# 128-token output tiles, early weighing of the last logit pair, and slot outputs replicated by their own products

## The chip, the cores and the metric

The kernel runs on one core of one Trainium2 chip. The time is device microseconds of one execution; the median of three executions of the kernel before is 542.49 us (540.43 to 543.66). The core's five engines run side by side, each in the order of its own instructions: TensorE (PE, products and their weight loads PEld), VectorE (DVE), ScalarE (ACT), GpSimd (POOL) and SyncE (SP, which only issues DMAs here). [...]

## The reference

Three layers in float32, with 2304 tokens (4 batches of 576) and a width of 512:

```
p_packed = attn(p, k, v);  a = attn(q, p_packed, p_packed)      # 8 heads, 32 packed queries
x   = a as tokens x 512
y   = sum_e prob[t, e] * (relu(x @ w1[e]) @ w2[e])              # 4 experts, hidden 1024
logits = y @ phi                                                # 32 slots
slot_in = softmax over tokens(logits).T @ y                     # 32 slots x 512
slot_out = relu(slot_in[e] @ m1[e]) @ m2[e]                     # 8 experts, 4 slots each
out = softmax over slots(logits) @ slot_out                     # 2304 x 512
```

The first softmax of the last layer runs over all 2304 tokens, so nothing behind slot_in can start before the last token's logits are known.

## The kernel before, in words

**Main loop.** It goes over batches b, four column blocks n of the hidden layer, halves kf and experts e (one step each, `sl`). A step makes h (L473, `mm1`), takes its relu into ht on ScalarE (L477), turns ht into hn on VectorE (L483, `flip_h`) and weighs hn with the experts' probabilities on GpSimd (L484). y itself is never formed: the logits are summed from ht with wphi = w2 @ phi (L500, `logits`), in two PSUM tiles lg, one for each pair pr of experts, and the slot sums are taken over hn (`pool_slots`, L611, tile sl) and meet w2 only at the end. ORDER writes down in which order a step issues its parts; in the last step it is logits, softmax, flip, attention, slot sums.

**Softmax of a batch.** `softmaxes(b)` is a generator, advanced by one `yield` a step: transposes of the two lg tiles into ls (L529), one multiplication of ls by the probabilities (L530), fold products that add the experts (L544, tile lt, PE), transposes into lt (L550), row maximum (L555), running maximum m_run and its negation nm (L557, L563), exponential with row sums (L565), transpose into dpt (L572). With dpt the slot sums of this batch can run. Between two of the last steps 16 products of the identity (L939, "warm") are put on TensorE.

**The stream of weights.** Chunks of w2 (16), m1 (32) and m2 (16, then 16 of 384 columns and 4 of 128 columns) are loaded in this order by SyncE (`load_chunk`, L715), each into the next of 39 buffers. The last 16 of these lie in hn, the input of the last slot sums, and come free piece by piece (ENDS) as `pool_slots(3, ...)` runs. Up to eight loads are under way at a time.

**The last part**, in order: slot sums sl of the last batch and their addition into tacc (L631); transposes tt (L961) and slot inputs si = tt @ w2 (L989); hid = relu(si @ m1) (L1026), between whose products `turn_c` prepares the combination weights ct, split into a high and a low part so that products in float32r keep their accuracy; transposes of hid into hm (L1047, L1049), where zeros keep the experts apart; so = hm @ m2 (L1074, `project`): once for experts 0 to 3 in all 512 columns, then for experts 4 to 7 in 384 columns and in 128 columns. The two are added on VectorE (L1094), a product with the selector matrix sel (L1096) places the 32 slots four times into 128 rows, a copy and a subtraction (L1098, L1099) make rr, whose lower 64 rows hold the rounding rest. An output tile is ct @ rr (L1112) for 96 tokens, drained by ScalarE and VectorE in turn (L1065), and stored with SyncE (L1119): 12 stores of 96 partitions by two rows of 384 columns, then 4 of 96 partitions by six rows of 128 columns, 288 KB each.

Of the kernel before, what the change touches and what calls it, by code (L numbers as in the profile page):

```python
# [18 lines left out]
def tile_packed_attention_moe_softmoe(  # L19
# [32 lines left out]
    NJ = NBLK // 3  # L52
# [65 lines left out]
    m_run = const.tile([128, NB], F32, name="m_run")  # L118
# [91 lines left out]
    def selectors(sel):  # L210
        for c in range(4):
            for s in range(2):
                pool.tensor_copy(
                    sel[:, 32 * c + 16 * s : 32 * c + 16 * s + 16].rearrange(
                        "p (x s) -> p x s", x=4
                    ),
                    ident.rearrange("p (x r) -> p x r", x=4)[:, :, 4 * s : 4 * s + 4],
                )
# [301 lines left out]
    def softmaxes(b):  # L520
# [5 lines left out]

        ls = sx(f"ls{b}", blocks)
        for pr in range(2):
            dve.transpose(out=ls[:, halves[pr], :], in_=wide(lg_t.pop((b, pr))))  # L529
        dve.tensor_tensor(  # L530
            out=ls, in0=ls,
            in1=dpe[:, b].rearrange("p r x -> p (r x)").unsqueeze(2).to_broadcast(blocks),
            op=ALU.mult,
        )
        yield
        own = slice(32 * b, 32 * b + 32)
        cc = c_sb[own]
        lt = sx(f"lt{b}", blocks)
        pss = []
        for hf in range(2):  # L540
            ps = tr_ps(f"lt{b}{hf}")
            r = slice(64 * hf, 64 * hf + 64)
            for pr in range(2):
# [11 lines left out]
        dve.tensor_reduce(out=mx, in_=flat, axis=AX.X, op=ALU.max)  # L555
        if b:
            dve.tensor_tensor(  # L557
                out=m_run[:, b : b + 1], in0=mx, in1=m_run[:, b - 1 : b], op=ALU.max
            )
        else:  # L560
            dve.tensor_copy(m_run[:, 0:1], mx)
        nm = small.tile([128, 1], F32, tag="nm", name=f"nm{b}", bufs=1)
        dve.tensor_scalar_mul(nm, m_run[:, b : b + 1], -1.0)  # L563
# [73 lines left out]
    def turn_c(ct):  # L637
        cf = soft.tile([128, S], F32, tag="sx", name="cf", bufs=2).rearrange(
            "p (x t) -> p x t", t=32
        )  # L640
        dve.transpose(out=cf, in_=c_sb)
        for b in range(NB):
            own = slice(32 * b, 32 * b + 32)
            for y0, ny in ((0, 2), (2, 1)):
                m = ny * NJ * 32
                ps = tr_ps(f"ct{b}{y0}")
# [5 lines left out]
                src = ps[:, :m].rearrange("p (y j t) -> p y j t", y=ny, t=32)  # L652
                dst = ct[:, b].rearrange("p j (t y) -> p y j t", y=3)[:, y0 : y0 + ny]
                for y in range(ny):
                    act.copy(dst[:, y], src[:, y])
                    for r in (slice(32, 64), slice(96, 128)):
                        dve.tensor_tensor(
                            out=dst[r, y], in0=src[r, y],
                            in1=dst[r, y].bitcast(F32), op=ALU.subtract,
                        )  # L660
                yield

    chunks = []
    for x in range(0, NFT, 2):
        for e in range(NE):
            chunks.append(
                w2[e, 128 * x : 128 * x + 256, :].rearrange("(x p) d -> p x d", p=128)
            )
# [4 lines left out]
    for x in range(0, NFT, 2):  # L673
        for e in range(4):
            chunks.append(
                m2[e, 128 * x : 128 * x + 256, :].rearrange("(x p) d -> p x d", p=128)
            )
    for d0, dw in PARTS:
        nx = CHUNK // dw
        for x in range(0, NFT, nx):  # L680
            for e in range(4):
                chunks.append(
                    m2[4 + e, 128 * x : 128 * (x + nx), d0 : d0 + dw].rearrange(
                        "(x p) d -> p x d", p=128
                    )
                )
# [50 lines left out]
    with tc.manual_schedule():  # L737
# [88 lines left out]
        flq = None  # L826
# [17 lines left out]
        for sl in range(nslot + 1):  # L844
# [62 lines left out]
            def step_logits():  # L907
                nonlocal sm_gen
# [40 lines left out]
        sel = rest(0)[:, :128]  # L949
        selectors(sel)  # L950
# [4 lines left out]
        ct = fin.tile([128, NB, NJ, 96], F32R, name="ct")  # L955
        for i in range(2):
            ps, ps2 = tr_ps(f"tt{i}a"), tr_ps(f"tt{i}b")
            for j in range(4):
                o = 128 * (4 * (2 * i + j // 2) + j % 2)
                for el in range(2):  # L960
                    pe.transpose(  # L961
                        (ps if j < 2 else ps2)[:, 256 * (j % 2) + 128 * el :][:, :128],
                        tacc[:, o + 256 * el : o + 256 * el + 128],
# [47 lines left out]
        cgen = turn_c(ct)  # L1011
# [31 lines left out]
        for i in range(2):  # L1043
            ps = tr_ps(f"hidt{i}")
            for j in range(4):
                o = 512 * i + 128 * j
                pe.transpose(ps[:, 128 * j : 128 * j + 128], hid[:, o : o + 128], ident)  # L1047
            for s in range(2):
                (act.copy if i else dve.tensor_copy)(  # L1049
                    hm[s][:, 4 * i : 4 * i + 4, :, 4 * s : 4 * s + 4].rearrange(  # L1050
                        "p a b c -> p (a b) c"
                    ),
                    ps.rearrange("p (a c) -> p a c", c=32)[:, :, 4 * s : 4 * s + 4],
# [13 lines left out]
        def project(so, s, dw):  # L1067
            nonlocal ck
            nx = CHUNK // dw
            for x in range(0, NFT, nx):  # L1070
                cks = [chunk_t.pop(ck + e) for e in range(4)]
                for xl in range(nx):
                    for e in range(4):
                        pe.matmul(  # L1074
                            so[32 * e : 32 * e + 32, :dw],
                            hm[s][:, x + xl, e, :],
                            cks[e][:, dw * xl : dw * xl + dw],
                            start=(x + xl == 0),
                            stop=(x + xl == NFT - 1),
                            tile_position=(0, 32 * e),  # L1080
                        )
# [3 lines left out]

        so = mm_ps("so")
        project(so, 0, DM)
        so_sb = rest(3)[:, :DM]
        act.copy(so_sb, so)
        for d0, dw in PARTS:  # L1090
            so = mm_ps(f"so{d0}")
            project(so, 1, dw)
            h = slice(d0, d0 + dw)
            dve.tensor_tensor(out=so_sb[:, h], in0=so[:, :dw], in1=so_sb[:, h], op=ALU.add)  # L1094
            sr = tr_ps(f"sr{d0}")
            pe.matmul(sr[:, :dw], sel, so_sb[:, h], start=True, stop=True)  # L1096
            rr = fin.tile([128, dw], F32R, name=f"rr{d0}")
            act.copy(rr, sr[:, :dw])  # L1098
            dve.tensor_tensor(  # L1099
                out=rr[64:128], in0=sr[64:128, :dw], in1=rr[64:128].bitcast(F32),  # L1100
                op=ALU.subtract,
            )
            nb, nt = 512 // dw, min(CHUNK // dw, NJ)
            for b in range(NB):
                rows = out[b * S : (b + 1) * S, h].rearrange("(r j) d -> r j d", j=NJ)
                for j0 in range(0, NJ, nt):
                    ob = out_tile()
                    for j in range(j0, j0 + nt, nb):
                        m = min(nb, j0 + nt - j)
                        ps = mm_ps(f"o{d0}_{b}_{j}")  # L1110
                        for jl in range(m):
                            pe.matmul(  # L1112
                                ps[:96, dw * jl : dw * jl + dw], ct[:, b, j + jl, :], rr,
                                start=True, stop=True,
                            )
                        drain(
                            ob[:96, dw * (j - j0) : dw * (j - j0 + m)], ps[:96, : dw * m]
                        )
                    (act if (d0, b) == (PARTS[-1][0], NB - 1) else sp).dma_start(  # L1119
                        rows[:, j0 : j0 + nt, :],  # L1120
                        ob[:96, : dw * nt].rearrange("p (j d) -> p j d", d=dw),
                    )
# [30 lines left out]
```

## Time and profile before

| | |
|---|---|
| median of three executions | 542.49 us |
| profiled execution | 541.67 us, span 539.6 us |
| busy, share of the span | PE 92%, DVE 56%, ACT 44%, POOL 46% |
| last fifth of the span | see the DMA line of the rows below |
| HBM read and written | 98.52 and 4.72 MB |
| chain that ended last | PE 65%, DVE 11%, DMA 8%, ACT 8% |

The page gives averages over the span: a busy share of 92% says nothing of the last 100 us by itself. A DMA share can exceed 1, since the times of packets that overlap on one engine are added. "Idle before" is the time in which an engine had nothing to do before an instruction, with what ended it.

### The profile page before, as it was taken

Reading aid. Unit: us, or ns where it says so; the run is one execution under the profiler, and the core shown is the slowest. Engines: PE = TensorE matmul, PEld = TensorE weight load, DVE = VectorE, ACT = ScalarE, POOL = GpSimd, SP = SyncE. Lnnn points to the kernel's source line nnn. Section 1 sums busy time; section 2 is a strip of 40 time slices with the busy share of each in tenths; the row PEclk is TensorE's granted clock in tenths of the full one; section 3 lists DMA queues with packets and bytes.
Section 4 is the critical chain, followed back from the end, with each engine's and each line's share of the span. In section 5 each row is a group of like instructions: output and inputs, shape, how many; then the busy total and the mean of one; then the engine's idle time right before and its main releaser. Section 6 shows DMA issues by size and latency. Waiting matters only on the chain.

```text
span 539.6 us, 12853 instructions
## 1 busy us (share of the span) xinstructions
PE 497.0 (92%) x5356; PEld 346.1 (64%) x5356; DVE 300.1 (56%) x559; ACT 240.0 (44%) x548; POOL 248.5 (46%) x310
## 2 busy tenths in 40 slices
PE   6898999999999999999998999999999887998883
PEld 5776787877865777877556777865878753222132
DVE  6265555747767575569755756567545425360051
ACT  3857464656452457455234565541454312120041
POOL 8412446697632667795236486732565512000000
PEclk9999999999999999999999999999999997998996
DMA  8998156253430443624215422640686459999998
GB/s 277 366 373 295 53 165 193 84 170 106 137 117 1 149 145 107 217 82 126 76 44 178 150 80 79 223 169 2 199 296 249 153 205 412 408 388 382 368 251 241
DMA packets 70873, 104.06 MB, mean 193 GB/s; under 512 B 4432, under 2 KB 50256, under 8 KB 70816
## 3 DMA queue, kind: packets, MB, share of 16 engines
q1 hardware_dynamic: 66992, 93.20, 50.2%
q0 software_dynamic: 3232, 9.75, 5.8%
q8 instruction: 42, 0.69, 0.5%
q10 hardware_dynamic: 592, 0.29, 0.2%
q14 instruction: 15, 0.12, 0.1%
HBM read 98.52 MB, written 4.72 MB: 191 GB/s over the span
## 4 chain that ended last, share of the span: by engine, by line
PE 65%; DVE 11%; DMA 8%; ACT 8%; issue 3%; POOL 3%; SPq 0%; POOLq 0%; DVEq 0%; ACTq 0%
PE h L473 30%; PE sl L611 7%; PE lg L500 5%; PE g L443 5%; DMA hn<-in_moe_w_dram 3%; ACT etm L336 3%; PE hid L1026 3%; PE pv L346 3%; PE sb L297 3%; PE sa L297 2%; DMA k<-in_k_dram 2%; DMA ck<-in_moe_w_dram 2%; PE si L989 1%; DVE hn L483 1%; PE w2t L251 1%
## 5 line engine op out<-in xcount | busy, mean ns | idle before, releaser
L473 PE MATMUL h<-a,g 128*128 128x288 f32 x1536 | 226.0, 301 | 2.5 <-POOL a L410 1.5
L473 PEld LDWEIGHTS h<-a,g 128*128 128x128 f32 x1536 | 208.0, 188 | 28.3 <-issue 22.3
L484 POOL TENSOR_TENSOR hn<-hn,dp_sb 128x576 f32<-128x576 f32 x128 | 151.6, 1191 | 123.1 <-DVE hn L483 118.8
L477 ACT ACTIVATE ht<-h 128x288 f32<-128x288 f32 x256 | 103.7, 412 | 149.1 <-PE h L473 148.8
L483 DVE STREAM_TRANSPOSE hn<-ht 128x576 f32<-128x576 f32 x128 | 96.6, 760 | 56.6 <-ACT ht L477 56.5
L455 DVE TENSOR_TENSOR g<-g,g 128x512 fp32r<-128x512 f32 x64 | 41.1, 684 | 26.6 <-ACT g L454 26.6
L611 PE MATMUL sl<-hn,dpt 32*32 32x512 f32 x1152 | 48.1, 597 | 2.3 <-DVE dpt L572 2.0
L454 ACT CAST g<-g 128x512 fp32r<-128x512 f32 x64 | 34.3, 588 | 21.1 <-PE g L443 21.0
L500 PE MATMUL lg<-ht,wphi 128*32 128x288 f32 x512 | 37.8, 412 | 0.0
L443 PE MATMUL g<-w,gl 64*32 64x512 f32 x512 | 35.7, 601 | 0.4 <-ACT ht L477 0.2
L611 PEld LDWEIGHTS sl<-hn,dpt 32*32 32x32 f32 x1152 | 21.0, 103 | 22.3 <-issue 13.3
L500 PEld LDWEIGHTS lg<-ht,wphi 128*32 128x32 f32 x512 | 13.5, 109 | 32.7 <-issue 25.5
L346 PE MATMUL pv<-etm,v 128*64 128x64 f32 x468 | 19.0, 225 | 6.7 <-ACT etm L336 2.0
L410 POOL TENSOR_TENSOR a<-a,a 64x576 fp32r<-64x576 f32 x14 | 19.9, 1424 | 9.6 <-ACT a L409 8.9
L336 ACT COPY etm<-et 32x288 f32<-32x288 f32 x52 | 22.3, 428 | 2.3 <-DVE et L330 1.1
L346 PEld LDWEIGHTS pv<-etm,v 128*64 128x64 f32 x468 | 16.2, 137 | 10.7 <-ACT etm L336 5.6
L1074 PE MATMUL so<-hn,tacc 128*32 128x384 f32 (+1 forms) x80 | 18.4, 586 | 2.7 <-DMA hn<-in_moe_w_dram 2.7
L378 DVE STREAM_TRANSPOSE nat<-sb 128x288 f32<-128x288 f32 x14 | 6.8, 483 | 25.3 <-PE sb L297 25.3
L629 DVE TENSOR_TENSOR tacc<-sl,tacc 128x512 f32<-128x512 f32 (+2 forms) x32 | 15.3, 544 | 9.4 <-PE sl L611 9.4
L256 ACT COPY hn<-w2t 128x512 f32<-128x512 f32 x32 | 17.2, 589 | 6.0 <-PE w2t L251 5.9
L251 PE MATMUL w2t<-ident,hn 128*128 128x128 f32 x128 | 17.5, 279 | 2.4 <-ACT hn L256 1.6
L631 DVE SCALAR_TENSOR_TENSOR tacc<-tacc,rsc,sl 128x384 f32<-128x384 f32 (+2 forms) x20 | 9.2, 527 | 17.3 <-PE sl L611 17.3
(180 smaller groups left out, 506.6 us busy)
## 6 DMA issues: line engine op xcount, KB each, us to landing
w<-in_moe_w_dram SPq DMA_DIRECT2D x32, 1024.0 KB, 5.3
hn<-in_moe_w_dram SPq DMA_DIRECT2D x42, 512.0 KB, 9.8
ck<-in_moe_w_dram SPq DMA_DIRECT2D x42, 512.0 KB, 9.0
hn<-in_moe_w_dram SPq DMA_DIRECT2D x14, 384.0 KB, 8.5
q<-in_q_dram POOLq DMA_DIRECT2D x12, 288.0 KB, 3.2
out_dram<-ob SPq DMA_DIRECT2D x11, 288.0 KB, 4.4
k<-in_k_dram POOLq DMA_DIRECT2D x10, 288.0 KB, 3.3
v<-in_v_dram POOLq DMA_DIRECT2D x10, 288.0 KB, 3.4
```

Source lines behind the costliest of these rows:

```text
L297: pe.matmul(ps[:, :HS], lhs[:, j, :], t[:, :, j, :], start=(j == 0), stop=(j == 1))
L336: act.copy(etb[hf % len(etb)][r, h % 2, :, 32 * (h // 2) : 32 * (h // 2) + 32], et[r, HB * hf : HB * hf + HB, :],)
L346: pe.matmul(pv[64 * par : 64 * par + 64, :64], vn[:, x, :], etb[hf % len(etb)][:, par, x, :], start=(hf == 0 and x == 0), stop=(hf == 1 an ...
L443: pe.matmul(pss[g][32 * ((c + 2 * g) % 4) : 32 * ((c + 2 * g) % 4) + 32, :], gl[b % 2][r, c, :], t[r, c], start=True, stop=True, tile_posi ...
L454: act.copy(hi, pss[g])
L455: dve.tensor_tensor(out=lo, in0=pss[g], in1=hi.bitcast(F32), op=ALU.subtract)
L473: pe.matmul(ps[:, :HS], gg[:, l, g, e % 2, fs], r[:, ts], start=(g == 0 and t == 0), stop=(g == 1 and t == 2),)
L477: act.activation(out=ht[:, ts], in_=ps[:, :HS], func=AF.Relu)
L483: dve.transpose(out=own, in_=unturned.pop((n, kf, e)).rearrange("p (x t) -> p x t", t=32))
L484: pool.tensor_tensor(out=own, in0=own, in1=dp_sb[:, n // NU, :, e].unsqueeze(2).to_broadcast([128, NBLK, 32]), op=ALU.mult,)
L500: pe.matmul(lg_t[b, pr][32 * c : 32 * c + 32, :HS], wphi[:, 2 * i + kf, 32 * e : 32 * e + 32], ht_t[n, kf, e][:, HS * hf : HS * hf + HS], ...
L611: pe.matmul(pss[f][c : c + 32, :], dpt[r, x, :], hn[r, p0 : p0 + NU, x, 2 * ep : 2 * ep + 2].rearrange("p n e k f -> p n (e k f)"), start= ...
```

## The change

- `softmaxes` of the last batch begins when the first lg tile is complete: pair 0 is transposed and multiplied then (`weigh`, `times`), pair 1 after the last logits; the fold products of pair 0 stand ahead of those of pair 1 in TensorE's order. The running maximum is kept negated (n_run), in one instruction. The last batch's exponential and its transpose into dpt are made in two halves, and its row sum is a reduction on VectorE behind them.
- The chunks of w2 and of m2 place rows differently: partition p takes neighbouring rows of the matrix (of m2 the rows 8p to 8p+7, in pieces). The transposes of tacc and hid take columns with a step of 2 or 8 to fit.
- hm holds each slot column four times, so that `project` gives the 128 rows that the selector product gave. Both groups of experts add up in the same two PSUM tiles (sos), which makes the first `project` two products (384 and 128 columns) instead of one of 512. The addition, so_sb and the selector product go. rr is made by a copy (rh) and one operation with a mask per partition (`lows`, 0 or -1), and ct likewise, with the matrix `perm` in place of fold.
- A partition now holds 18 neighbouring tokens of the output; ct has 128 columns a product. There are 9 stores of 128 partitions by two rows of 384 columns and 3 of 128 by six rows of 128 columns, 384 KB each.

```diff
-    NJ = NBLK // 3
+    OUT_X = {384: 2, 128: 6}
...
-    def selectors(sel):
+    def spread(perm, lows):
+        to = perm.rearrange("p (e c s i) -> p e c s i", e=4, c=4, s=2)
+        src = fold[:, 0].rearrange("p (s e i) -> p s e i", s=2, e=4)
         for c in range(4):
             for s in range(2):
...
+                pool.tensor_copy(to[:, :, c, s, :], src[:, s])
+        for k, w in enumerate((16, 32)):
+            dve.tensor_reduce(
+                out=lows[:, k : k + 1],
+                in_=ident.rearrange("p (a b) -> p a b", b=w)[:, :, w // 2 :],
+                axis=AX.XY, op=ALU.add,
+            )
+        dve.tensor_scalar_mul(lows, lows, -1.0)
...
+        last = b == NB - 1
         ls = sx(f"ls{b}", blocks)
...
         own = slice(32 * b, 32 * b + 32)
         cc = c_sb[own]
         lt = sx(f"lt{b}", blocks)
+
+        def weigh(pr):
+            dve.transpose(out=ls[:, halves[pr], :], in_=wide(lg_t.pop((b, pr))))
+
+        def times(prs):
+            xs = slice(halves[prs[0]].start, halves[prs[-1]].stop)
+            dve.tensor_tensor(
+                out=ls[:, xs], in0=ls[:, xs],
+                in1=dpe[:, b, prs[0] : prs[-1] + 1].rearrange("p r x -> p (r x)")
+                .unsqueeze(2).to_broadcast([128, HB * len(prs), 32]),
+                op=ALU.mult,
+            )
+
         pss = []
...
+
+        def folded(pr):
+            for hf in range(2):
+                if not pr:
+                    pss.append(tr_ps(f"lt{b}{hf}"))
+                r = slice(64 * hf, 64 * hf + 64)
                 pe.matmul(
-                    ps[:, :HS], fold[r].rearrange("p c t -> p (c t)"), ls[r, halves[pr], :],
+                    pss[hf][:, :HS], fold[r].rearrange("p c t -> p (c t)"),
+                    ls[r, halves[pr], :],
                     start=(pr == 0), stop=(pr == 1), tile_position=(64 * hf, 0),
                 )
-            pss.append(ps)
+
+        if last:
+            weigh(0)
+            times((0,))
+            yield "first"
+            weigh(1)
+            times((1,))
+            folded(0)
+        else:
+            weigh(0)
+            weigh(1)
+            times((0, 1))
+        yield
+        if not last:
+            folded(0)
+        folded(1)
...
+        nm = n_run[:, b : b + 1]
         if b:
-            dve.tensor_tensor(
-                out=m_run[:, b : b + 1], in0=mx, in1=m_run[:, b - 1 : b], op=ALU.max
+            dve.scalar_tensor_tensor(
+                out=nm, in0=mx, scalar=-1.0, in1=n_run[:, b - 1 : b],
+                op0=ALU.mult, op1=ALU.min,
             )
         else:
...
+            dve.tensor_scalar_mul(nm, mx, -1.0)
         sm = small.tile([128, 1], F32, tag="lsm", name=f"lsm{b}", bufs=1)
-        act.activation(out=flat, in_=flat, func=AF.Exp, bias=nm, accum_out=sm)
+        if last:
+            for x in halves:
+                act.activation(out=lt[:, x], in_=lt[:, x], func=AF.Exp, bias=nm)
+        else:
+            act.activation(out=flat, in_=flat, func=AF.Exp, bias=nm, accum_out=sm)
         rs = None
         if b:
             rs = small.tile([128, 1], F32, tag="rsc", name=f"rsc{b}", bufs=1)
-            act.activation(out=rs, in_=m_run[:, b - 1 : b], func=AF.Exp, bias=nm)
+            act.activation(
+                out=rs, in_=n_run[:, b - 1 : b], func=AF.Exp, bias=nm, scale=-1.0
+            )
         yield
         dpt = soft.tile([128, NBLK, 32], F32, tag="dpt", name=f"dpt{b}", bufs=1)
-        dve.transpose(out=dpt, in_=lt)
+        for x in halves if last else (slice(0, NBLK),):
+            dve.transpose(out=dpt[:, x], in_=lt[:, x])
+        if last:
+            dve.tensor_reduce(out=sm, in_=flat, axis=AX.X, op=ALU.add)
...
+            for x0 in range(0, NBLK, HB):
+                m = HB * 32
+                ps = tr_ps(f"ct{b}{x0}")
                 pe.matmul(
-                    ps[:, :m], fold[own].rearrange("p c t -> p (c t)"),
-                    cf[own, NJ * y0 : NJ * (y0 + ny), :],
+                    ps[:, :m], perm[own], cf[own, x0 : x0 + HB, :],
                     start=True, stop=True, tile_position=(32 * b, 0),
                 )
...
+                src = ps[:, :m].rearrange("p (x t) -> p x t", t=32)
+                dst = ct[:, x0 : x0 + HB, own]
+                act.copy(dst, src)
+                dve.scalar_tensor_tensor(
+                    out=dst, in0=dst.bitcast(F32), scalar=lows[:, 0:1], in1=src,
+                    op0=ALU.mult, op1=ALU.add,
+                )
...
-                m2[e, 128 * x : 128 * x + 256, :].rearrange("(x p) d -> p x d", p=128)
+                m2[e].rearrange("(p x) d -> p x d", x=NFT)[:, x : x + 2, :]
...
+                    m2[4 + e, :, d0 : d0 + dw].rearrange("(p x) d -> p x d", x=NFT)[
+                        :, x : x + nx, :
+                    ]
...
+                    if ln == NB * NU - 1 and lk == 0:
+                        sm_last = softmaxes(NB - 1)
+                        next(sm_last)
                     if ln % NU == NU - 1 and lk == 1:
-                        sm_gen = softmaxes(ln // NU)
+                        sm_gen = sm_last if ln == NB * NU - 1 else softmaxes(ln // NU)
...
+                    hm[s][:, 4 * i : 4 * i + 4].rearrange(
+                        "p a b (c u) -> p (a b) c u", u=8
+                    )[:, :, :, 4 * s : 4 * s + 4],
+                    ps.rearrange("p (a c) -> p a c", c=32)[:, :, 4 * s : 4 * s + 4]
+                    .unsqueeze(2).to_broadcast([128, 16, 4, 4]),
...
-        def project(so, s, dw):
+        sos = [
+            ps_lg.tile([128, 512], F32, tag="lg", name=f"so{d0}")[:, :dw] for d0, dw in PARTS
+        ]
+
+        def project(s, n, w, parts):
             nonlocal ck
-            nx = CHUNK // dw
-            for x in range(0, NFT, nx):
+            for x in range(0, NFT, n):
                 cks = [chunk_t.pop(ck + e) for e in range(4)]
...
+                for xl in range(n):
+                    for so, o, dw in parts:
+                        for e in range(4):
+                            pe.matmul(
+                                so[32 * e : 32 * e + 32],
+                                hm[s][:, x + xl, e, :],
+                                cks[e][:, w * xl + o :][:, :dw],
+                                start=(s == 0 and x + xl == 0),
+                                stop=(s == 1 and x + xl == NFT - 1),
+                                tile_position=(0, 32 * e),
+                            )
                 ck += 4
...
+        project(0, 2, DM, [(so, *pt) for so, pt in zip(sos, PARTS)])
+        for so, (d0, dw) in zip(sos, PARTS):
+            project(1, CHUNK // dw, dw, [(so, 0, dw)])
             h = slice(d0, d0 + dw)
...
+            rh = fin.tile([128, dw], F32R, name=f"rh{d0}")
             rr = fin.tile([128, dw], F32R, name=f"rr{d0}")
...
+            act.copy(rh, so)
+            dve.scalar_tensor_tensor(
+                out=rr, in0=rh.bitcast(F32), scalar=lows[:, 1:2], in1=so,
+                op0=ALU.mult, op1=ALU.add,
+            )
+            nb, nt = 512 // dw, OUT_X[dw]
+            rows = out[:, h].rearrange("(p x) d -> p x d", x=NBLK)
+            for x0 in range(0, NBLK, nt):
+                ob = out_tile()
+                for x in range(x0, x0 + nt, nb):
+                    m = min(nb, x0 + nt - x)
+                    ps = mm_ps(f"o{d0}_{x}")
+                    for xl in range(m):
+                        pe.matmul(
+                            ps[:, dw * xl : dw * xl + dw], ct[:, x + xl, :], rr,
+                            start=True, stop=True,
                         )
...
+                    drain(ob[:, dw * (x - x0) : dw * (x - x0 + m)], ps[:, : dw * m])
+                (act if d0 and x0 + nt == NBLK else sp).dma_start(
+                    rows[:, x0 : x0 + nt, :],
+                    ob[:, : dw * nt].rearrange("p (x d) -> p x d", d=dw),
```

## Rows read from the trace of the kernel before

**Rows 1.** The page's 40 equal slices: busy tenths of the DMA engines.
```profile
DMA  8998156253430443624215422640686459999998
```

**Rows 2.** Stretches: from:to, length, busy us (instructions) per engine, clock, DMA share, GB/s.
```profile
420.00:428.00 8.00, 8.00 (x68) 7.04 (x66) 3.38 (x6) 3.35 (x9) 4.88 (x5) 1.00 0.37 133
436.00:439.00 3.00, 3.00 (x100) 1.64 (x84) 0.00 (x0) 0.00 (x0) 0.00 (x0) 1.00 0.02 5
446.00:472.00 26.00, 21.30 (x150) 8.49 (x154) 12.02 (x39) 4.46 (x13) 4.86 (x5) 0.87 1.03 410
476.00:493.00 17.00, 15.47 (x107) 4.90 (x109) 6.40 (x15) 3.47 (x9) 0.00 (x0) 0.90 1.05 386
497.00:509.00 12.00, 10.22 (x47) 2.23 (x46) 0.00 (x0) 0.59 (x1) 0.00 (x0) 1.00 1.07 373
513.00:518.00 5.00, 3.50 (x15) 0.81 (x14) 0.56 (x1) 0.26 (x1) 0.00 (x0) 1.00 0.98 260
518.00:521.00 3.00, 2.09 (x9) 1.32 (x9) 2.02 (x4) 1.77 (x5) 0.00 (x0) 1.00 0.59 161
522.00:532.00 10.00, 8.63 (x103) 6.12 (x101) 5.77 (x14) 5.59 (x12) 0.00 (x0) 0.92 0.98 297
534.00:538.00 4.00, 0.00 (x0) 0.00 (x0) 0.00 (x0) 0.00 (x0) 0.00 (x0) 0.50 0.92 235
```

**Rows 3.** TensorE's weight loads, 490 to 515 us: us waited, times, longest.
```profile
PEld so L1074 <- DMA hn<-in_moe_w_dram: 12.1, 14, 1.3
...
PEld so L1074 <- DMA ck<-in_moe_w_dram: 3.8, 5, 1.2
```

**Rows 4.** SyncE's waits, 405 to 445 us: us waited, times, longest.
```profile
SPq L715 <- PE sl L611: 8.7, 1, 8.7
```

**Rows 5.** Chain of waits from the last logits to dpt: start, us, what.
```profile
429.35 0.49 DVE ls L529
...
429.86 0.77 DVE ls L530
...
430.68 1.25 PE lt L544 x8
...
431.95 0.86 DVE lt L550 x2
...
433.61 0.17 DVE m_run L557
...
433.81 0.17 DVE nm L563
...
434.00 0.88 ACT lt L565 x2
...
434.89 0.79 DVE dpt L572
```

**Rows 6.** Chain of waits behind the last 384-wide weight: start, us, what.
```profile
514.59 1.49 PE so L1074 x10
...
516.18 0.57 DVE hn L1094
...
516.79 0.93 PE sr L1096 x2
```

**Rows 7.** Instructions in order of time, 425 to 449 us: start, us, what, idle.
```profile
427.73 0.44 DVE L529 STREAM_TRANSPOSE ls<-lg 128x288 f32<-128x288 f32 x1
...
428.17 0.41 ACT L477 ACTIVATE ht<-h 128x288 f32<-128x288 f32 x1 [0.39 <-PE h L473]
...
430.54 0.77 DVE L483 STREAM_TRANSPOSE hn<-ht 128x576 f32<-128x576 f32 x1
...
431.39 1.19 POOL L484 TENSOR_TENSOR hn<-hn,dp_sb 128x576 f32<-128x576 f32 x1 [2.32 <-DVE hn L483]
...
438.22 10.51 SPq L715 DMA_DIRECT2D hn<-in_moe_w_dram  x12
```

**Rows 8.** Instructions in order of time: the output products of the 384 columns.
```profile
518.87 6.37 PE L1112 MATMUL o<-rr,ct 128*96 128x384 f32 x24 [1.16 <-DVE rr L1099]
```

More of the change, by code (lines that the diff above doesn't have):

```diff
@@ L525, in wide @@
             return ps[:, :HS].rearrange("p (x t) -> p x t", t=32)
+        last = b == NB - 1
         ls = sx(f"ls{b}", blocks)
-        for pr in range(2):
-            dve.transpose(out=ls[:, halves[pr], :], in_=wide(lg_t.pop((b, pr))))
-        dve.tensor_tensor(
[L531 to L535, printed above, removed]
         own = slice(32 * b, 32 * b + 32)
@@ L643, in turn_c @@
             own = slice(32 * b, 32 * b + 32)
-            for y0, ny in ((0, 2), (2, 1)):
-                m = ny * NJ * 32
-                ps = tr_ps(f"ct{b}{y0}")
+            for x0 in range(0, NBLK, HB):
+                m = HB * 32
+                ps = tr_ps(f"ct{b}{x0}")
                 pe.matmul(
-                    ps[:, :m], fold[own].rearrange("p c t -> p (c t)"),
-                    cf[own, NJ * y0 : NJ * (y0 + ny), :],
+                    ps[:, :m], perm[own], cf[own, x0 : x0 + HB, :],
                     start=True, stop=True, tile_position=(32 * b, 0),
                 )
[L652 to L660, printed above, removed]
+                src = ps[:, :m].rearrange("p (x t) -> p x t", t=32)
[5 more added lines that the diff above has]
+                )
                 yield
@@ L825, in tile_packed_attention_moe_softmoe @@
         post, lgq = [], []
-        flq = None
+        flq, sm_last = None, None
         sm_gen, att_gens, ready, soon = None, [], -1, 0
@@ L907, in step_logits @@
             def step_logits():
-                nonlocal sm_gen
+                nonlocal sm_gen, sm_last
                 if sl < 4:
@@ L948, in tile_packed_attention_moe_softmoe @@
         fin = ctx.enter_context(tc.tile_pool(name="fin", bufs=1, reuse_waits="tile"))
-        sel = rest(0)[:, :128]
-        selectors(sel)
+        perm = rest(0)[:, :128]
+        lows = small.tile([128, 2], F32, tag="lows", name="lows", bufs=1)
+        spread(perm, lows)
         st2 = [rest(1 + i).rearrange("p (c x s) -> p c x s", c=2, s=32) for i in range(2)]
@@ L1010, in tile_packed_attention_moe_softmoe @@
             )
-        cgen = turn_c(ct)
+        cgen = turn_c(ct, perm, lows)
         for s in range(2):
@@ L1045, in tile_packed_attention_moe_softmoe @@
             for j in range(4):
-                o = 512 * i + 128 * j
-                pe.transpose(ps[:, 128 * j : 128 * j + 128], hid[:, o : o + 128], ident)
+                pe.transpose(
+                    ps[:, 128 * j : 128 * j + 128],
+                    hid.rearrange("p (f x) -> p x f", x=NFT)[:, 4 * i + j],
+                    ident,
+                )
             for s in range(2):
                 (act.copy if i else dve.tensor_copy)(
[L1050 to L1053, printed above, removed]
+                    hm[s][:, 4 * i : 4 * i + 4].rearrange(
[3 more added lines that the diff above has]
+                    .unsqueeze(2).to_broadcast([128, 16, 4, 4]),
                 )
@@ L1084, in project @@
                     load_chunk()
[L1086 to L1092, printed above, removed]
+        project(0, 2, DM, [(so, *pt) for so, pt in zip(sos, PARTS)])
+        for so, (d0, dw) in zip(sos, PARTS):
+            project(1, CHUNK // dw, dw, [(so, 0, dw)])
             h = slice(d0, d0 + dw)
-            dve.tensor_tensor(out=so_sb[:, h], in0=so[:, :dw], in1=so_sb[:, h], op=ALU.add)
-            sr = tr_ps(f"sr{d0}")
-            pe.matmul(sr[:, :dw], sel, so_sb[:, h], start=True, stop=True)
+            rh = fin.tile([128, dw], F32R, name=f"rh{d0}")
@@ L1097, in tile_packed_attention_moe_softmoe @@
             rr = fin.tile([128, dw], F32R, name=f"rr{d0}")
[L1098 to L1101, printed above, removed]
-            )
[L1103 to L1117, printed above, removed]
-                        )
[L1119 to L1122, printed above, removed]
```

40 lines of the change are left out of this document (7 added, 33 removed).

## The prediction

> **What bounds the kernel now.** I read the 40-slice page line first, then busy time by stretch of the last 120 us, then the queues' waits, then the chain of waits in two places. The DMA line is broken up until about slice 31 and then stands at 8 to 9 to the end [rows 1]: in the last fifth the transfers are the limit, not the engines. The stretches say it more sharply [rows 2]. From 446 to 472 us the DMA engines are busy 1.03 of the time at 410 GB/s, from 476 to 493 at 386, from 497 to 509 at 373, and from 522 to 532 they write the output at 297. TensorE is busy too, but it waits for the weights: in "so" its weight loads wait 12.1 + 3.8 us for DMA [rows 3]. So TensorE has about 15 us in hand before the last weight lands, and what is saved or lost on it between 446 and 500 us moves nothing. The granted clock of 0.87 from 446 to 472 [rows 2] costs nothing for the same reason: the transfers run at their full 1.03 meanwhile.
>
> Two holes stand in this stream. From 436 to 439 us the DMA share is 0.02 [rows 2], since SyncE, which issues the loads in order, waits 8.7 us for the first piece of sl (L611) to free buffers in hn [rows 4]. sl starts only when a serial chain, from the last logits at 429.35 us to dpt at 435.69, is through [rows 5]. The second hole is 518 to 521 us, share 0.59 [rows 2]: the weights are in and the first output isn't there yet [rows 6].
>
> So four things can pay: the chain before sl, the rate of the stream, the hole before the first store, and the rate of the stores.
>
> **Part 1, the chain before sl.** Step by step against [rows 5]:
> - The multiplication L530 has both pairs in one instruction, 0.77 us. Pair 0 is transposed (0.44) ahead of the chain already, at 427.73 [rows 7]; its multiplication now joins it four steps earlier, while VectorE is busy 3.38 of 8 us [rows 2] and waits for ScalarE's next ht anyway. What is left is pair 1, 288 columns: at least half, 0.38, at most 0.77; I take 0.42.
> - The fold on TensorE (L544) is 8 matmuls in 1.25 us. The four of pair 0 run during pair 1's multiplication; four are left, between 0.63 and 1.25; I take 0.70. Behind the multiplication VectorE also has the last flip of hn (L483, 0.77 [rows 7]), as now. It would end at 429.35 + 0.48 + 0.45 + 0.79 = 431.07, the fold at 431.02. So the lt transposes start at 431.07 instead of 431.95: 0.88 saved, and the flip is level with the fold, so that a faster fold would give no more.
> - The running maximum and its negation are one instruction instead of two of 0.17: 0.19 with the gap.
> - The exponential and the transpose are cut into halves, and the row sum leaves ScalarE. sl takes its first nine columns from the first half alone. Now 0.88 + 0.02 + 0.79 = 1.69; then half an exponential, by the 288-wide activation 0.41 (L477), and half a transpose, 0.44 (L529) [rows 7]: 0.87. Saved 0.82. If sl had to wait for both halves, another 0.41 would go and 0.41 be left.
> Together 1.9 us (1.4 to 2.2). It reaches the stream: SyncE's first hn load moves from 438.22 [rows 7] to 436.3, into the hole in which no transfer runs. GpSimd's last multiplication of hn (1.19 us from 431.39 [rows 7]) ends before sl, then as now, and isn't on this path.
>
> **Part 2, longer rows.** The chunks of w2 and of the first half of m2 take two neighbouring rows to a partition, 4 KB in one piece, instead of two pieces of 2 KB. w2's are loaded mostly before the main loop ends, where the DMA line has holes [rows 1]: nothing. The 16 chunks of m2 (8.39 MB) lie in the full stream. m1's rows are 4 KB already and run at 410, m2's 2 KB rows at 386 [rows 2]: 21.7 us becomes 20.5, 1.3 us saved. Bounds: 1.3, and below nothing, since each partition now starts 16 KB from the next, which no row here shows (a rival). The last 20 chunks keep pieces of 1536 and 512 B.
>
> **Part 3, from the last weight to the first store.** Gone are the addition L1094 (0.57), the selector product L1096 (0.93) and their gaps; the copy and the subtraction into rr stay as a copy and one masked operation of the same width [rows 6]. So the first store is issued about 1.6 us earlier after the last 384-wide weight. But it can't use more than what the DMA engines have idle: 0.41 of the 3 us from 518 to 521 [rows 2], 1.2 us. I take 1.2, bounds 0 (the hole stays, for a reason of the transfers themselves) and 1.6. Beyond it the store queues behind the 512-byte weights.
>
> **Part 4, the stores.** 4.72 MB leave in 12 stores of 128 partitions instead of 16 of 96. They are the limit from 522 us on: 0.98 busy at 297 GB/s with 1536-byte pieces, 235 with 512-byte ones at the thin end [rows 2]. No row shows a store from 128 partitions. The bounds are the same rate (0 us) and the rate at which 128 partitions read in pieces of the same size: 373 for 1536 B, 260 for 512 B [rows 2]. 3.54 MB take 11.9 or 9.5 us, 1.18 MB 5.0 or 4.5: 2.4 + 0.5, with 0.2 off for the thin end, 2.7. I take the reading rate: it is the row with the same pieces at a full share, and besides the direction the 96 partitions are the one difference. The products and drains keep up: 24 products in 6.37 us [rows 8] filled 12 stores, one each 0.53 us, against 1.0 us to write one (295 KB at 297).
>
> Behind cover: the wider copies into hm (four times the elements), the 128-column second product of each step, the strided weight loads of the transposes, the shorter ct, and spread() on VectorE and GpSimd all lie between 446 and 500 us, under TensorE's 15 us. Were that gone, they would cost about 1 us.
>
> **Sum.** 1.9 + 1.3 + 1.2 + 2.7 = 7.1 us. The profiled execution took 541.67 us (span 539.6 and 2.1 around it); it becomes 534.6. It lay 0.8 under the median of the three shown (542.49), so I put the median to come half-way, at 535.0.
>
> **Rivals.**
> - *Stores no faster.* Their rate is set by the writes and part 4 is 0: 537.3. For it: the pieces keep their size, and a share of 0.98 at 297 means that a written piece holds its engine longer than a read one [rows 2]. Against: nothing in these rows ties that to writing rather than to the 96 partitions.
> [...]
> - *The pitch gives part 2 back and stores stay.* 1.9 + 1.2 = 3.1: 538.6.
> - *Little arrives.* sl waits for both halves, parts 2, 3 and 4 are nothing: 541.67 - 1.5 = 540.2.
> - *Slower: the 16 KB pitch of m2.* All 36 m2 chunks (8.39 + 6.29 + 2.10 MB) now have neighbouring partitions 16 KB apart. They take 21.7 + 16.9 + 8.1 = 46.7 us at the rates of now. The other parts bring 5.8; if this stretch runs 11% slower, nothing is left, at 15% it costs 8.2 and the time is 544.1. For it: no row has this pitch. Against: m1's rows, one each 4 KB, and m2's, one each 2 KB, run within 6% of one another in the same stream, 410 and 386 [rows 2]. [...]
>
> **Chances.** Forecast 0.45, partition groups 0.12, stores no faster 0.22, pitch gives back 0.09, little arrives 0.05, slower 0.07. The range 532.0 to 539.5 reaches from the partition groups with a microsecond for the runs' own spread to the pitch case; the last two are outside. A change under 0.5% (2.7 us) can't be told from none in this kernel; "little arrives" (0.05), a third of the pitch case (0.03) and half of "slower" (0.03) lie there: faster 0.85, same 0.11, slower 0.04.
>
> **What would show it.** Right: sl starts within 4.2 to 4.9 us of the end of the last logits, not 6.5; the first hn load follows it; the stretch with m2's first half shows about 410 GB/s; no dip of the DMA share between the last weights and the first store; stores at 370 GB/s. Wrong: TensorE in "so" no longer waiting for DMA (then the cover is gone), a rate under 330 anywhere in m2, or stores still at 297. A time above 540 would mean that the stream isn't the limit I take it for.

## The result, and the profile after

The changed kernel takes 534.26 us (median of four runs, 533.26 to 534.84); the kernel before took 541.6 beside it. The ratio is 0.9859, with a 95% interval of 0.982 to 0.9897. The forecast was 535.0. The profiled execution took 533.26 us, its span is 531.5 instead of 539.6. Lines of code have moved: sl is now L648, the loads L749, so L1120, the output products L1151, the stores L1156.

The page's 40 slices, DMA engines in tenths and GB/s:

```profile
DMA  8999145343430353443204424351368459999998
GB/s 280 367 373 312 47 151 190 113 151 102 158 126 1 116 182 105 151 155 115 90 2 149 152 93 141 121 209 71 120 224 332 159 192 367 409 408 408 374 326 288
```

As before [rows 1] the line is broken up until slice 33 and full from slice 34 on; the prediction read the border at slice 31, which changed nothing, since it took its rates from the stretches. The same stretches, moved with the last logits (columns as in [rows 2]):

```profile
443.80:469.80 26.00, 21.32 (x150) 8.54 (x154) 10.96 (x38) 3.93 (x12) 4.84 (x5) 0.87 1.03 409
473.00:490.00 17.00, 15.27 (x140) 6.08 (x136) 3.42 (x7) 2.74 (x7) 0.00 (x0) 0.90 1.02 408
493.00:505.00 12.00, 9.99 (x63) 2.84 (x62) 0.00 (x0) 0.00 (x0) 0.00 (x0) 1.00 1.07 373
509.00:514.00 5.00, 3.31 (x17) 1.16 (x16) 0.85 (x2) 0.89 (x3) 0.00 (x0) 1.00 1.12 280
514.00:517.00 3.00, 2.95 (x12) 1.85 (x11) 2.83 (x6) 2.70 (x7) 0.00 (x0) 1.00 1.10 331
517.00:524.00 7.00, 5.40 (x87) 4.40 (x85) 3.21 (x7) 3.07 (x7) 0.00 (x0) 1.00 1.05 375
526.00:530.00 4.00, 0.00 (x0) 0.00 (x0) 0.00 (x0) 0.00 (x0) 0.00 (x0) 0.50 0.90 251
```

Read against [rows 2]: the m1 stretch is the same (409 GB/s, it was 410). m2's first half runs at 408 instead of 386, the 384-column weights at 373 as before. Where the share fell to 0.59 it is now 1.10. The stores write at 375 instead of 297.

The chain before sl, from the chain of waits (start, us, what), to be laid beside [rows 5]:

```profile
428.73 0.49 DVE ls L538
...
429.24 0.47 DVE ls L542
...
429.75 0.81 PE lt L556 x4
430.56 0.84 DVE lt L578 x2
...
432.21 0.17 DVE n_run L586
...
432.40 0.54 ACT lt L595
...
432.97 0.49 DVE dpt L607
...
433.60 9.74 PE sl L648 x273
```

From the first transpose to sl it is 4.87 us; it was 6.47. Two lines of the instructions in order of time say what the transposes waited for, and that sl (433.60) didn't wait for the second half of dpt, which was ready at 432.97 + 0.90 = 433.87:

```profile
430.54 0.85 DVE L578 STREAM_TRANSPOSE lt<-lt 128x288 f32<-128x288 f32 x2 [0.15 <-PE lt L556]
...
432.97 0.90 DVE L607 STREAM_TRANSPOSE dpt<-lt 128x288 f32<-128x288 f32 x2 [0.60 <-ACT lt L595]
```

And the way behind the last 384-wide weight, to be laid beside [rows 6]:

```profile
510.42 1.49 PE so L1120 x10
...
511.94 0.49 ACT rh L1138
...
512.45 0.62 DVE rr L1139
...
513.11 0.46 PE o L1151
```

The first output product starts 2.7 us after the start of this "so"; it was 518.87 - 514.59 = 4.3 [rows 6, rows 8]. From the start of this "so" to the end of the span it was 539.6 - 514.6 = 25.0 us [rows 6]; now it is 531.5 - 510.4 = 21.1. TensorE still waits for the weights (us in total, times, longest), 12.9 us in "so" after 15.9 in [rows 3]; so most of the cover that the prediction counted on is still there:

```profile
PEld so L1120 <- DMA hn<-in_moe_w_dram: 11.0, 14, 1.2
...
PEld so L1120 <- DMA ck<-in_moe_w_dram: 1.9, 2, 0.9
```

### The profile page after: what moved, and what is told of

It reads as the page before. It is cut to its first block, busy times and chain, and to the rows that moved or that the text cites. A ratio compares the mean times of both kernels' runs of the same rounds, so it can differ in the third digit from the quotient of the medians.

```text
span 531.5 us, 12898 instructions
## 1 busy us (share of the span) xinstructions
PE 492.4 (93%) x5404; PEld 347.1 (65%) x5404; DVE 293.1 (55%) x539; ACT 235.6 (44%) x539; POOL 247.9 (47%) x310
## 4 chain that ended last, share of the span: by engine, by line
PE 65%; DMA 13%; ACT 8%; DVE 8%; issue 3%; POOL 3%; SPq 0%; POOLq 0%; DVEq 0%; ACTq 0%
PE h L477 32%; PE sl L648 7%; DMA ck<-in_moe_w_dram 7%; PE lg L504 6%; PE g L447 5%; DMA hn<-in_moe_w_dram 3%; ACT etm L340 3%; PE sa L301 3%; PE pv L350 3%; PE sb L301 3%; DMA k<-in_k_dram 2%; PE o L1151 1%; PE w2t L255 1%; POOL hn L488 1%; PE pw L241 1%
## 5 line engine op out<-in xcount | busy, mean ns | idle before, releaser
L648 PE MATMUL sl<-hn,dpt 32*32 32x512 f32 x1152 | 48.2, 597 | 1.5 <-DVE dpt L607 1.2
L458 ACT CAST g<-g 128x512 fp32r<-128x512 f32 x64 | 34.3, 588 | 21.1 <-PE g L447 21.0
L648 PEld LDWEIGHTS sl<-hn,dpt 32*32 32x32 f32 x1152 | 21.0, 103 | 21.4 <-issue 11.0
L1120 PE MATMUL so<-hn,tacc 128*32 128x384 f32 (+1 forms) x104 | 18.2, 492 | 2.6 <-DMA hn<-in_moe_w_dram 2.6
L301 PE MATMUL sa<-k,pt 128*128 128x288 f32 x56 | 16.7, 425 | 1.9 <-DVE k L292 1.4
```

The costliest lines, as they stand in the source:

```text
L301: pe.matmul(ps[:, :HS], lhs[:, j, :], t[:, :, j, :], start=(j == 0), stop=(j == 1))
L458: act.copy(hi, pss[g])
L648: pe.matmul(pss[f][c : c + 32, :], dpt[r, x, :], hn[r, p0 : p0 + NU, x, 2 * ep : 2 * ep + 2].rearrange("p n e k f -> p n (e k f)"), start= ...
```

## The experiments

Times are medians; the ratio is to the kernel before, run beside each. The changed kernel has 0.9859.

**Part 1 alone, in the kernel before.** `softmaxes`, n_run and the early start are those of the changed kernel, the rest is that of the kernel before.

```diff
...
+                    if ln == NB * NU - 1 and lk == 0:
+                        sm_last = softmaxes(NB - 1)
+                        next(sm_last)
...
```

> The kernel before with the early weighing, the one-instruction maximum and the halved exponential alone; loads and stores stay. Theory (the stream waits for the last slot sums): sl starts 1.6 us sooner after the last logits, as in the changed kernel, the first hn load follows by the same, and the time falls by 1.6 us (ratio 0.997). Rival (the transfers are limited by something else than the start of sl): the chain is shorter by 1.6 us but the last weight lands at the same distance from the last logits as before, and the time stays (ratio 1.000).

539.89 us, ratio 0.9969 (0.9953 to 0.9985): 1.7 us less. Its chain of waits has sl 4.88 us behind the first transpose, and its transfers (stretches) are those of the kernel before:

```profile
428.61 0.50 DVE ls L534
...
432.86 0.49 DVE dpt L603
...
433.49 2.52 PE sl L644 x64
```

```profile
473.50:490.50 17.00, 15.48 (x109) 4.95 (x109) 6.34 (x15) 3.46 (x9) 0.00 (x0) 0.90 1.05 386
515.50:518.50 3.00, 1.79 (x9) 1.15 (x8) 1.71 (x4) 1.73 (x4) 0.00 (x0) 1.00 0.55 155
519.50:529.50 10.00, 8.73 (x104) 6.21 (x103) 5.95 (x14) 5.70 (x13) 0.00 (x0) 0.95 0.98 297
```

The hole of 0.55 and the 297 GB/s are still there, only earlier. The first hn load is issued 2.40 us after the start of sl (435.89), as before (438.22 [rows 7], sl 435.82). So the chain's 1.6 us go through to the end, as the theory said.

**Part 2 taken back, in the changed kernel.**

```diff
-                m2[e].rearrange("(p x) d -> p x d", x=NFT)[:, x : x + 2, :]
+                m2[e, 128 * x : 128 * x + 256, :].rearrange("(x p) d -> p x d", p=128)
...
```

> The changed kernel with the 16 chunks of m2's first half back in two pieces of 2 KB to a partition; hid is transposed once for each layout, 8 more transposes under TensorE's cover. Theory (piece size sets the rate): these chunks go at 386 instead of 408 GB/s, the time rises by 1.3 us against the changed kernel (to about 535.5). Rival (the gain of these chunks was only the earlier start): no difference, 534.3.

536.05 us, ratio 0.9887 (0.9863 to 0.991). The intervals of this run and of the changed kernel overlap, so the stretches have to decide:

```profile
444.00:470.00 26.00, 20.91 (x146) 7.99 (x150) 11.04 (x37) 3.47 (x11) 5.07 (x5) 0.87 1.03 410
476.00:492.00 16.00, 14.85 (x164) 6.59 (x152) 3.02 (x7) 2.44 (x6) 0.00 (x0) 1.00 1.05 387
```

m2's first half is back at 387 GB/s, all else as in the changed kernel. The 16 loads take 21.8 us from landing to landing, against 20.5: 1.3 us, as expected.

**Part 3 taken back, in the changed kernel.**

```diff
+            so_sb = rest(3)[:, h]
+            dve.tensor_copy(so_sb, so)
+            sr = tr_ps(f"sr{d0}")[:, :dw]
+            pe.matmul(sr, ident, so_sb, start=True, stop=True)
-            act.copy(rh, so)
+            act.copy(rh, sr)
...
```

> The changed kernel with the removed way between so and rr put back: a copy on VectorE and a product with the identity on TensorE ahead of rh (0.57 + 0.93 us and gaps). Theory (the transfers idle until the first store is there): the first store is issued 1.6 us later, a dip of the DMA share below 0.9 comes back between the last weights and the stores, and the time rises by 0.6 to 1.2 us (about 535.2). Rival (the 512-byte weights last until then anyway, the way was covered): no dip, the time stays within 0.3 us of 534.3.

535.49 us, ratio 0.9879 (0.9857 to 0.99), again with overlapping intervals. The stretches show the dip:

```profile
514.00:516.00 2.00, 2.00 (x8) 1.67 (x8) 1.21 (x3) 1.37 (x3) 0.00 (x0) 0.59 0.56 143
516.00:524.00 8.00, 6.85 (x88) 5.30 (x87) 4.41 (x10) 3.58 (x9) 0.00 (x0) 0.89 1.02 362
```

For 2 us the DMA engines are busy at 0.56, and from the landing of the last 384-wide load to the end it is 22.2 us instead of 21.1. So the shorter way is worth 1.1 us, by the trace.

**Stores cut by partitions, and cut by rows.** Two kernels, each with 24 stores of 192 KB.

By partitions:

```diff
+                for p0 in (0, 64):
+                    r = slice(p0, p0 + 64)
...
+                        rows[r, x0 : x0 + nt, :],
+                        ob[r, : dw * nt].rearrange("p (x d) -> p x d", d=dw),
```

By rows:

```diff
+                for x in range(x0, x0 + nt, nt // 2):
+                    o = dw * (x - x0)
...
+                        rows[:, x : x + nt // 2, :],
+                        ob[:, o : o + dw * nt // 2].rearrange("p (x d) -> p x d", d=dw),
```

> The changed kernel with each store cut into one of partitions 0 to 63 and one of 64 to 127, 192 KB each, 24 instead of 12. Theory A (a store's time is set by the partitions that crowd one group): a store of half the partitions costs nearly what a whole one does, about 0.97 us, so the writing takes 9 to 12 us more (about 544). Theory B (only pieces and bytes count, or the number of stores a little): 374 GB/s as now, at most 1 us more (534 to 535.5).

> The changed kernel with each store cut by rows instead: all 128 partitions, half the rows, 192 KB each, 24 instead of 12, the same pieces of 1536 and 512 bytes. It is the control of the cut by partitions. Theory A and theory B: 374 GB/s as now, within 1 us of the changed kernel (534 to 535.3). If a fixed cost for each store set the rate, it would rise by several us here as well.

By partitions 540.23 us, ratio 0.9973 (0.9955 to 0.999); by rows 532.51, 0.9827 (0.9808 to 0.9846). The stretch of the 384-column stores, first by partitions, then by rows:

```profile
518.00:526.00 8.00, 5.03 (x86) 4.13 (x85) 3.08 (x7) 2.98 (x6) 0.00 (x0) 0.95 0.87 268
```

```profile
517.00:524.00 7.00, 5.16 (x86) 4.25 (x85) 3.20 (x7) 3.02 (x7) 0.00 (x0) 1.00 1.03 371
```

268 against 371 GB/s for the same pieces, sizes and number. But the share of 0.87 says that the DMA engines were not full, and SyncE's own rows suggest why (duration of one issue in ns, least, median, most; first by partitions, then by rows):

```profile
L1158 SPq DMA_DIRECT2D out_dram<-ob x14: 595/601/774, 515.2 to 533.8; - x14
```

```profile
L1158 SPq DMA_DIRECT2D out_dram<-ob x14: 368/442/1174, 514.1 to 526.3; - x14
```

A store from 64 partitions took 0.6 us to issue, even the first, with no store queued ahead of it. Three in a row took 1.94 us, and 192 KB each 0.65 us are 300 GB/s: issuing may have been the limit of the rate. What issuing can't explain is how long the pieces hold their engines: the share divided by the rate is engine time per byte, and 0.87 / 268 is 17% more than 1.03 / 371. So pieces from 64 partitions take longer; what that alone does to the rate this pair leaves open.

**The same number of stores from 64 partitions, and from 96.**

From 64, where r is 0 to 63 and 64 to 127 in turn:

```diff
...
+                    dst = rows[r, k : k + 4, :]
+                    src = ob[r, dw : 2 * dw].unsqueeze(1).to_broadcast([64, 4, dw])
...
```

Of 96:

```diff
+                r = slice(0, 128 if d0 else 96)
...
```

> The changed kernel with eight of its nine stores of 384 columns made of 64 partitions by four rows instead of 128 by two: as many stores, bytes and pieces, issued at the same points, but in turn from partitions 0 to 63 and 64 to 127. The four rows of a store all take the values of one, so this part of the output is not the reference's. Theory A (a store's time is set by the partitions that crowd one group): these stores go at little over half of 374 GB/s, and the time rises by 4 to 9 us. Theory B (only pieces, bytes and the number of stores count): no change, 534.3. It takes away what spoke against the run by 64 partitions, where SyncE's issues, 0.6 us for 192 KB, could have been the limit.

> The changed kernel with its nine stores of 384 columns cut to partitions 0 to 95; the last 32 partitions' tokens are not stored in these columns, a quarter of these bytes. Theory A: a store of 96 costs what a store of 128 does, about 1.0 us, its rate falls from 374 GB/s to about 290, and the time stays within 0.7 us of 534.3 although less is written. Theory B: each store costs a quarter less, and the time falls by about 2.2 us (532.1).

64 by 4: 538.75 us, ratio 0.9945 (0.9928 to 0.9963). Of 96: 532.01, 0.9825 (0.9797 to 0.9853). Stretches, in this order:

```profile
518.00:526.00 8.00, 5.10 (x86) 4.20 (x85) 3.15 (x7) 2.97 (x7) 0.00 (x0) 0.96 0.99 268
```

```profile
518.00:524.00 6.00, 4.78 (x85) 3.96 (x83) 2.81 (x7) 2.77 (x6) 0.00 (x0) 1.00 1.03 327
```

From 64 the share is now 0.99 and the rate still 268 GB/s: as many stores of the same size, in pieces of the same length, eight of them from half of the partitions, cost 4.5 us more. Issuing is not the limit here. But one thing besides the partitions has changed: the four rows of a store read the same 1536 bytes of ob four times, and the engine time per byte (0.99 / 268) is 32% above that of whole stores (1.05 / 375), where the cut by partitions, which reads nothing twice, had 17%. So about half of this excess may come from the repeated reading; no run separates the two. A store took 4.7 to 8.2 us from issue to landing, so stores from both halves were under way at once, and what one half alone can write isn't tested either.

Of 96, each piece holds its engine 12% longer (1.03 / 327), with every row read once. A fixed cost for each store would also make a smaller store slower per byte, but the cut by rows speaks against it: 192 KB from all 128 partitions at 371 GB/s. So theory B falls: the partitions count. Theory A in its strict form falls too: stores of 96 land 0.89 us apart, where A gave the 0.97 of whole stores and B three quarters of it, 0.73. The medians are 2.2 us apart, as B had said, but their intervals overlap; by the trace the way from the landing of the last 384-wide load to the end is 19.7 us instead of 21.1, so 1.4 us less, between the two theories. What holds is the order: 268 from 64, 327 from 96, 375 from 128 partitions.

**Distance of the rows in the output.** Stores of 96 wrote at 327 here and at 297 in the kernel before; their partitions lie 36 KB apart here and lay 12 KB apart there. One kernel gives the kernel before 36 KB, the other gives the changed one 12 KB.

In the kernel before:

```diff
+                if b < NB - 1:
+                    rows = out[: 3 * S, h].rearrange("(r y) d -> r y d", y=3 * NJ)
+                    rows = rows[:, NJ * b : NJ * (b + 1), :]
```

In the changed kernel:

```diff
...
+                y = 768 * (x0 // 6)
+                rows = out[y : y + 768, h].rearrange("(p x) d -> p x d", x=6)
...
```

> The kernel before with the stores of three of its four batches going to other rows: neighbouring partitions 36 KB apart in the output, as in the changed kernel, instead of 12 KB; the fourth batch stays. The rows of the output stand in another order, so it is not the reference's. The run with 96 of 128 partitions wrote at 330 GB/s, the kernel before at 297: the open question is what else differs. Theory (the distance of the rows): the first nine stores of 384 columns go at 330 GB/s, 0.89 us each, the last three at 1.02, and the time falls by 1.2 to 1.6 us (about 540.2). Rival (not the distance, but the number of stores or what runs beside them): all twelve stay at 1.02 us, 541.7.

> The changed kernel with neighbouring partitions 12 KB apart in the output instead of 36 KB, in three groups of 768 rows; all else stays. The rows of the output stand in another order, so it is not the reference's. Theory (the distance of the rows is a part of the gain): the stores fall from 374 to about 335 GB/s and the time rises by 1 to 1.5 us (535.5). Rival: 374 GB/s and 534.3 as now.

541.42 us, ratio 0.9996 (0.9979 to 1.0013), and 534.52, ratio 0.9857 (0.982 to 0.9895): neither moves. The stores' stretch in the first and in the second:

```profile
524.00:532.00 8.00, 6.89 (x94) 4.82 (x94) 4.74 (x11) 4.08 (x9) 0.00 (x0) 1.00 0.96 286
```

```profile
518.00:526.00 8.00, 6.46 (x91) 4.96 (x90) 4.38 (x10) 4.28 (x9) 0.00 (x0) 0.99 1.04 372
```

The far rows don't raise 297 (286 in this trace), and the near rows don't lower 375: the distance is not it. What makes the kernel before write at 297 where 96 partitions could do 327 stays open.

**Halves of 256 columns.** Can the 512-byte pieces at the end be avoided?

```diff
-    PARTS = ((0, 384), (384, 128))
-    OUT_X = {384: 2, 128: 6}
+    PARTS = ((0, 256), (256, 256))
+    OUT_X = {256: 3}
```

> The changed kernel with the last weights and the output split into 256 + 256 columns instead of 384 + 128: all their pieces are 1 KB, six stores of 128 partitions by three rows each. Theory (the transfers are the limit to the end, 1 KB pieces go at about 370 GB/s and 512-byte ones at 270): the last weights take 2.2 us less, the stores 1.2 us less, the first half's stores cover the second half's way from weight to store: about 531. Rival (the way from the last weight to the last store is the limit, and half of the output instead of a quarter now hangs on it): the same or up to 2 us slower, with a dip of the DMA share ahead of the last six stores.

534.26 us, ratio 0.986 (0.9839 to 0.988): no difference. Weights, the way to the second half, last stores (stretches):

```profile
502.00:514.00 12.00, 9.35 (x84) 4.91 (x80) 2.95 (x7) 3.60 (x7) 0.00 (x0) 0.90 1.09 349
...
521.00:524.00 3.00, 2.45 (x15) 1.97 (x15) 1.82 (x5) 2.09 (x4) 0.00 (x0) 1.00 0.65 224
524.00:530.00 6.00, 0.72 (x6) 0.45 (x4) 0.85 (x3) 1.13 (x3) 0.00 (x0) 0.86 1.04 347
```

The rival came out: the same time, and a dip ahead of the last six stores. 1 KB pieces came at 349 GB/s and not at the 370 of the theory, and the hole came back (0.65 for 3 us): the second half's first store was issued at 522.4, and the first half's last store landed at 524.4, so for a while too little was under way.

**By rows once more, beside the changed kernel once more.** No edit but that by rows.

> The stores by row once more, beside the changed kernel on the same chip, to see whether they are faster. If the first store may leave after one drain instead of two and the last one is half as long, 0.3 to 0.6 us less than the changed kernel; the earlier run showed 1.7 less, of which 1.0 us was a late landing of one chunk in the profile of the changed kernel alone. If that was chance, the two are within 0.6 us.

> The changed kernel as it is, to be compared with the run before it, and to see whether the first 128-column chunk lands 2.7 us behind the last 384-column one again or 1.7 us as in the other runs. If the late landing belongs to the kernel, 2.7 again; if it was chance, 1.7, and a span 0.9 us shorter from there on.

534.28 us, ratio 0.9861 (0.9836 to 0.9886), and 533.99, 0.9853 (0.9829 to 0.9877): no difference by the clock, so the 1.7 us of the first run by rows did not come again. The traces do differ: from the landing of the last 384-wide load to the end it is 20.3 us in both runs by rows and 21.0 to 21.1 in four traces with whole stores of 128 (the changed kernel twice, that with 2 KB pieces, that with near rows). These 0.8 us are less than the scatter of a whole run, and what makes them is not shown. The late landing of the first 128-column chunk was chance: 1.7 us behind the chunk ahead, not 2.7. But the span from the last 384-wide load on was 21.1 us again and not 0.9 shorter, so that expectation was wrong. The rates of m2 and of the stores came again (stretches):

```profile
473.00:490.00 17.00, 15.16 (x118) 5.95 (x121) 3.93 (x8) 3.14 (x8) 0.00 (x0) 0.90 1.03 409
...
517.00:524.00 7.00, 5.93 (x89) 4.62 (x88) 3.76 (x9) 3.68 (x8) 0.00 (x0) 1.00 1.05 377
```

By the clock, no kernel here that does the whole work was faster than the changed one more than once.

## Why the prediction was right

| step | forecast | measured |
|---|---|---|
| 1, chain before sl | 1.9 us | 1.6, the chain in all runs with it; 1.7 alone, by the clock |
| 2, 4 KB pieces in m2 | 1.3 | 1.3 (408 for 386 GB/s) |
| 3, way to the first store | 1.2 | 1.1 (taken back) |
| 4, stores from 128 partitions | 2.7 | 2.8 as the rest (25.0 - 21.1, less 1.1); not taken back alone |
| sum | 7.1 | 6.8 of the trace, 7.3 between the medians |

- **What bounds the kernel.** Right: part 1 alone goes through to the end (1.7 us by the clock), and parts 2 to 4, which save transfer time and idle time of transfers, do too. TensorE still waited 12.9 us in "so", so the work behind cover cost nothing that shows.
- **Part 1** was mis-sized by 0.3 us, in four steps by a little each: the halved exponential took 0.54 and not 0.41, the half transpose 0.49 and not 0.44, the multiplication 0.47 and not 0.42, the fold 0.81 and not 0.70. The one-instruction maximum was right (0.2 for 0.19). The row for the exponential was that of a relu of the same width. sl did start on the first half alone, 4.9 us behind the last logits, at the edge of the 4.2 to 4.9 that the prediction gave. The lt transposes waited for the fold, and not for the flip that the prediction had level with it.
- **Part 2**: the rate of the 4 KB pieces of m1 held for m2 (409 and 408 GB/s). The rival of the 16 KB distance fell: 408 and 373 GB/s with it.
- **Part 3**: the dip of the share went (0.59 before, 1.10 now), and came back with the longer way (0.56).
- **Part 4**: the stores reached the rate of the reads (375 and 373), as forecast. The reason given, that the 96 partitions are the one difference besides the direction, is shown in part: stores of 96 in the changed kernel wrote 327, so of the rise from 297 to 375 the part above 327 is the partitions'; the 30 GB/s below it stay open. On 3.54 MB the first is 1.4 us and the second 1.1. So that the forecast size came out whole is in part luck. The rival "stores no faster" fell. The partition groups, with 0.12 of the chances, are theory A of the experiments carried over to whole stores: one of 128 partitions would take what one of 96 did, so 12 stores would take 12/16 of the time of 16, which gave 533.1 and, a microsecond lower, the near end of the range. No run shows that: whole stores landed 0.97 us apart and those of 96 0.89. That the partitions count at all is shown (268 from 64, 327 from 96, 375 from 128); by what mechanism is not.
- **The span fell by 8.1 us, more than the 6.8 of the steps.** The last logits came at 428.70 instead of 429.32 us, and over the runs here, none of which edits the loop's products, they ended between 428.1 and 431.2, so these 0.6 us are scatter. The stretch from there to the landing of the last 384-wide load scatters between 81.3 and 82.9 us among kernels with the same loads; it was 85.2 before and is 81.7, 0.6 us more than parts 1 and 2 give. One profile's span is good to about a microsecond. By the clock, the interval of the ratio allows a gain of 5.6 to 9.7 us: that 7.1 and 7.3 lie so close is chance, and the steps rest on the traces.

## What to carry to other kernels

Where the stretches here showed a DMA share of 1.02 to 1.12, the bytes, the length of their pieces (408 GB/s with 4 KB, 373 with 1536 B) and the holes between them (shares of 0.02 and 0.59 in the kernel before, 3 us each) made the time, while TensorE waited 12.9 us in "so". In another kernel with such stretches, find each hole's releaser and shorten that chain, and leave the busy engines beside it alone. If stores end the kernel, an output tile that fills all 128 partitions is worth trying: stores from 128 wrote 375 GB/s here and stores from 96 wrote 327. When halving a wide instruction, don't halve its price (the multiplication went from 0.77 to 0.47 us, the transpose into dpt from 0.79 to 0.49); take the half's from a row of the same operation: the four halves here came out 0.3 us dearer together than estimated.

## What the runs showed of the hardware

- Stores of the same 1536-byte pieces wrote 375 GB/s from 128 partitions (DMA share 1.05) and 327 from 96 (1.03); the kernel before had 297 from 96 (0.98), for a reason that stays open. From 64 (0 to 63 and 64 to 127 in turn) it was 268 twice: at a share of 0.87, where issuing may have been the limit, and at 0.99, where each piece was read four times.
- Whether neighbouring partitions lay 12 or 36 KB apart in the output made no difference to stores of 128 partitions: 372 and 375 GB/s.
- SyncE took 0.60 us to issue a store of 64 partitions by two rows and, at the least, 0.37 for one of 128 by one row, the same bytes.
- Reading rates by piece in these last stretches, at a share of 1.02 to 1.12: 4 KB 408, 2 KB 387, 1536 B 373, 1 KB 349, 512 B 280 GB/s (the last with some 1536-byte pieces; 260 in the kernel before, at a share of 0.98).
